# Four block pairs of the second layer by Strassen's scheme instead of three, with the sums of its first matrix formed inside the first layer's loop

## The chip, the cores and the metric

One core of one Trainium2 chip runs the whole program. Its engines are TensorE (PE in the rows, its weight loads PEld), VectorE (DVE), ScalarE (ACT), GpSimd (POOL) and SyncE (SP), which here only issues DMAs. The metric is the device time of one execution in microseconds (us), the median of the runs.

## The reference: attention in chunks, then two feed-forward layers

```python
# attention: 8 batches x 8 heads, 576 positions in chunks of 64, head_dim 64
scores = scale * np.matmul(q_c, k_c.transpose(0, 1, 2, 4, 3))
scores = scores - np.max(scores, axis=-1, keepdims=True)
attn = np.exp(scores)
attn = attn / (np.sum(attn, axis=-1, keepdims=True) + 1e-09)
out = np.matmul(attn, v_c)
x = np.ascontiguousarray(attn_out.transpose(0, 2, 1, 3)).reshape(B * S, H * D)   # 4608 tokens x 512

# first layer: rational activation, d_ff 2048
h = x @ w_in
h2 = h * h
h3 = h2 * h
P = a[0] + a[1] * h + a[2] * h2 + a[3] * h3
Q = 1.0 + np.abs(b[0]) * np.abs(h) + np.abs(b[1]) * h2
g = P / (Q + 1e-06)
return (g @ w_out).astype(np.float32)

# second layer, d_ff 2048
h = x @ w_in
r = np.maximum(h, 0.0)
g = s * (r * r) + b
return (g @ w_out).astype(np.float32)
```

## The kernel before, in words

**Tiling.** The 4608 tokens are `NB` = 9 blocks of `TB` = 512; the model width 512 is `KD` = 4 slices of 128, the width 2048 is `MF` = 16 slices of 128. Every operand of a product is held as a sum of a high and a low part (`xh`, `xl`; `gh`, `gl`; the two halves of a weight tile), so that one product of two tiles is three matmuls. The weights come from memory as 64-bit words and are put together on the chip, tile by tile: `w_stage` loads one, `w_ends` (two ACT operations, `w` and `wst`), `w_clamp` and `w_shift` (DVE), `w_top` (DVE, reads `wst` and `w`), `w_sum` (POOL), `w_hi` (ACT) and `w_lo` (DVE or POOL).

**Steps.** A step i is one slice of 128 of one block: `mm1(i)` (12 matmuls of 512 columns into one of three PSUM banks `h`), the element-wise work, and, some steps later, `mm2(i)` (12 matmuls into the accumulators `acc`). Of the first layer's element-wise work `ew_abs`, `ew_num`, `ew_ln`, `ew_exp` and `ew_hi` are on ACT, `ew_den` (two operations, `r`) and `ew_lo` (`gl`) on POOL, `ew_b` (two operations, `t`) and `ew_d` (three operations, the last writes `t` again and frees the bank `h`) on DVE. The first layer has 9 x 16 = 144 steps, the second layer has 48 such plain steps for its first three blocks. The attention of 36 tiles of 128 tokens runs ahead of the blocks that need it, between the steps.

**The other six blocks** of the second layer go in three pairs by Strassen's scheme: seven products of half-size matrices in place of eight, in each of the two multiplications. For that the 2x2 parts of the weights have to be added and subtracted first; `conv` in `finish` does it for both matrices, 8 sets of two tiles each (`kind` 0 is the first matrix, `w_in`, `kind` 1 the second), and writes the results to memory (`wq_d`), from where `wi_load` and `wo_load` fetch them. A pair has 336 matmuls in each of its two multiplications.

**What sets the order.** Each engine works its own list in order. `START` is a list written out by hand, one token an operation, up to step 33 (`BEGUN`); it holds the conversion of the 32 tiles of the first layer's weights. Then a loop in code runs steps 33 to 127, the same for each step, with one attention tile every four steps. `TURN` is again a list, up to step 165, with the conversion of the 32 tiles of the second layer. From there `finish` lets a planner with costs and due times set the order of 26 plain steps, the 16 sets of `conv` and the three pairs.

## Time and profile before

| what | value |
|---|---|
| median of 3 runs (lowest to highest) | 1665.79 us (1664.94 to 1668.18) |
| the profiled execution: its time, its span | 1667.5 us, 1665.4 us |
| granted TensorE clock over the span | 0.989 |
| busy: PE, DVE, ACT, POOL | 96%, 79%, 66%, 41% |
| the chain that ended last | PE 85%, DVE 8%, ACT 2%, issue 2%, DMA 1%, POOL 1% |
| first matmul of steps 0, 33, 48, 128, 144, 166 | 56.8, 269.2, 359.0, 830.0, 912.8, 1038.0 us |

The last row is read from the timeline of PE: the start of the first matmul on line 460 of that step. So the program has five stretches: up to 56.8 us (attention of the first tiles, no step yet), `START` up to 269, the loop up to 830, `TURN` up to 1038, and what `finish` plans. The views used are the page, busy times by stretch (a stretch's length, then for each engine the busy time and in brackets the number of instructions, then the granted clock, the DMA share and GB/s), groups of instructions by line and shape (busy time, mean ns of one, idle time of the engine before them and its releaser), and waits.

### The profile page before, as it was taken

To read this page: it belongs to the slowest core of one execution; us is meant where nothing else is said; L and a number is where in the kernel's file an instruction comes from. 1 tells how busy PE (TensorE), PEld (TensorE's weight loads), DVE (VectorE), ACT (ScalarE), POOL (GpSimd) and SP (SyncE) were. 2 spreads that over 40 slices of the span, in tenths; PEclk is the share of its full clock that TensorE was granted. 3 is DMA by queue.
4 is the path that set the end of the run, shared out by engine and by line. 5 is a ranking of instruction groups with operands and counts; after the bars stand their busy time and mean duration, and the time that the engine had idled before them with its cause. 6 is when DMAs were issued, how large, how long until landed. Compare 5 with 4: busy or idle time off the path is not lost.

```text
span 1665.4 us, 26182 instructions
## 1 busy us (share of the span) xinstructions
PE 1604.4 (96%) x9148; PEld 1313.3 (79%) x9148; DVE 1311.4 (79%) x2071; ACT 1091.3 (66%) x1824; POOL 678.1 (41%) x576
## 2 busy tenths in 40 slices
PE   4689999999999999999999999899999999999997
...
GB/s 205 160 124 115 73 55 111 34 29 64 39 57 31 60 39 33 59 31 77 33 82 112 92 127 101 276 325 246 190 252 241 194 151 276 219 222 161 286 182 67
DMA packets 339971, 217.76 MB, mean 131 GB/s; under 512 B 262528, under 2 KB 297344, under 8 KB 339840
## 3 DMA queue, kind: packets, MB, share of 16 engines
...
## 4 chain that ended last, share of the span: by engine, by line
PE 85%; DVE 8%; ACT 2%; issue 2%; DMA 1%; POOL 1%; SPq 0%; DVEq 0%; ACTq 0%; POOLq 0%
PE acc L478 27%; PE ae L1041 12%; PE h L460 9%; PE h L461 9%; PE h L462 9%; PE hA L980 8%; PE hE L980 4%; PE hc L980 2%; PE hc L1041 2%; PE pat L350 1%; PE pat L289 1%; PE pat L325 1%; DVE h L607 1%; DVE t L608 1%; DVE ah L606 1%
## 5 line engine op out<-in xcount | busy, mean ns | idle before, releaser
L460 PE MATMUL h<-xh,w 128*128 128x512 f32 x768 | 308.6, 402 | 9.3 <-DVE t L608 5.2
L462 PE MATMUL h<-xh,w 128*128 128x512 f32 x768 | 301.7, 393 | 0.0
L461 PE MATMUL h<-xl,w 128*128 128x512 f32 x768 | 301.5, 393 | 0.0
L478 PE MATMUL acc<-gh,w 128*128 128x512 f32 x1152 | 285.5, 390 | 0.6 <-ACT gh L616 0.6
L478 PEld LDWEIGHTS acc<-gh,w 128*128 128x128 f32 x1152 | 215.7, 188 | 46.0 <-ACT gh L616 1.0
L1041 PE MATMUL ae<-gs,wo 128*128 128x512 f32 x864 | 219.4, 391 | 2.3 <-DVE acc L1062 1.2
L568 POOL TENSOR_SCALAR r<-ah,ab_sb 128x512 f32<-128x512 f32 x138 | 110.1, 798 | 235.4 <-ACT ah L551 235.1
L1041 PEld LDWEIGHTS ae<-gs,wo 128*128 128x128 f32 x864 | 161.8, 188 | 38.6 <-DVE acc L1062 2.4
L571 POOL TENSOR_TENSOR r<-r,ah 128x512 f32<-128x512 f32 x140 | 182.4, 1303 | 13.8 <-ACT r L566 2.2
L460 PEld LDWEIGHTS h<-xh,w 128*128 128x128 f32 x768 | 145.7, 190 | 43.2 <-DVE t L608 8.6
L622 POOL TENSOR_TENSOR gl<-t,gh 128x512 fp32r<-128x512 f32 x129 | 167.8, 1301 | 16.2 <-ACT gh L616 14.5
L462 PEld LDWEIGHTS h<-xh,w 128*128 128x128 f32 x768 | 145.3, 189 | 31.3
L461 PEld LDWEIGHTS h<-xl,w 128*128 128x128 f32 x768 | 145.8, 190 | 29.0 <-DVE xl L366 0.5
L606 DVE SCALAR_TENSOR_TENSOR ah<-r,h 128x512 f32<-128x512 f32 x144 | 98.3, 683 | 79.3 <-ACT h L599 78.7
L478 PE MATMUL acc<-gl,w 128*128 128x512 f32 x576 | 154.2, 390 | 0.0
L980 PE MATMUL hA<-xs,wi 128*128 128x512 f32 x576 | 146.7, 390 | 0.7 <-ACT g L991 0.7
L616 ACT ACTIVATE gh<-t 128x512 fp32r<-128x512 f32 x144 | 90.8, 631 | 78.0 <-DVE t L608 71.4
L406 POOL TENSOR_TENSOR w<-w,wst 128x512 int32<-128x512 int32 x64 | 94.6, 1487 | 79.2 <-DVE w L403 48.5
L980 PEld LDWEIGHTS hA<-xs,wi 128*128 128x128 f32 x576 | 108.0, 188 | 23.7 <-ACT g L991 1.1
L478 PEld LDWEIGHTS acc<-gl,w 128*128 128x128 f32 x576 | 108.1, 188 | 22.6 <-POOL gl L622 0.3
L599 ACT ACTIVATE h<-ah,exb 128x512 f32<-128x512 f32 x144 | 99.5, 691 | 39.1 <-DVE t L590 36.6
L594 ACT ACTIVATE ah<-r,lnb 128x512 f32<-128x512 f32 x144 | 103.4, 718 | 30.3 <-POOL r L571 29.8
...
## 6 DMA issues: line engine op xcount, KB each, us to landing
wi<-wq SPq DMA_DIRECT2D x84, 512.0 KB, 4.1
wo<-wq SPq DMA_DIRECT2D x84, 512.0 KB, 4.7
...
wst<-in_moe_w_out_dram SPq DMA_DIRECT2D x30, 512.0 KB, 4.6
wst<-in_moe_w_in_dram SPq DMA_DIRECT2D x29, 512.0 KB, 5.1
...
```

Of the source, the lines that this page charges most:

```text
L460: T.matmul(h, wh, xh[:, kk], start=kk == 0, stop=False)
L461: T.matmul(h, wh, xl[:, kk], start=False, stop=False)
L462: T.matmul(h, wl, xh[:, kk], start=False, stop=kk == KD - 1)
L478: T.matmul(o, l, r, start=first and n == 0, stop=last and n == 2)
L568: eng.tensor_scalar(out=r, in0=ah, scalar1=ab_sb[:, 1:2], scalar2=ab_sb[:, 0:1], op0=ALU.mult, op1=ALU.add)
L571: eng.tensor_tensor(out=r, in0=r, in1=ah, op=ALU.mult)
L594: A.activation(tmp[i]["ah"], tmp[i]["r"], AF.Ln, scale=RS, bias=lnb)
L599: A.activation(h_t[i], tmp[i]["ah"], AF.Exp, scale=-1.0, bias=exb)
L606: V.scalar_tensor_tensor(out=t, in0=r, scalar=ONE, in1=y, op0=ALU.add, op1=ALU.mult)
L622: (eng or (G if i < N1 else V)).tensor_tensor(out=gl, in0=tmp.pop(i)["g"], in1=f(g_t[i][0]), op=ALU.subtract)
L980: T.matmul(ps[b], w[:, l, z * P:(z + 1) * P], x[:, z], start=n == 0 and p in (1, 2, 5), stop=n == 5, skip_group_check=True)
L1041: T.matmul(o, w[:, e, l, dp * P:(dp + 1) * P], gx[t, 2 * u + e, k][0][:, g], start=n == 0 and p in (1, 2, 5), stop=n == 5, skip_group_chec ...
```

## The change

- `finish` begins at step 150 and has 10 plain steps in place of 26; the second layer has 16 plain steps (block 0 alone) instead of 48, and four pairs (blocks 1 and 2 to 7 and 8) instead of three.
- The first layer's order of steps: block 0 with slices 0 to 7, block 1 with 0 to 7, block 2 with all 16, block 1 with 8 to 15, block 0 with 8 to 15, then blocks 3 to 8. Since three blocks' inputs are alive at once, that of block 0 is written to memory (`x_out`) and read back (`x_back`).
- `START` reaches to step 48; it and `TURN` are new lists, in which the parts of `att_S_out`, `att_sum`, `w_mid`, `ew_b` and `ew_d` are tokens of their own. `TURN` converts 16 weight tiles, those of `w_out`, not 32, and fetches the 16 tiles of `w_in` (`w_get`).
- The loop of steps 48 to 127 is now `LOOP`, a list of 16 steps, played five times. It holds, beside the 16 steps and four attention tiles, the conversion and the sums of two sets (four tiles) of the second layer's `w_in` (`pre_load` to `pre_put2`). There are 8 sets, so four of five passes begin two each, and the last third of a pass's second set falls into the next pass. In `LOOP` three of 16 `ew_lo` and one of four `att_norm` go to DVE (`yD`, `nD`), and three of 16 first operations of `ew_den` to ACT (`rP`).
- `conv` is left for `kind` 1 alone.

```diff
-BEGUN = 33
+BEGUN = 48
-TURN_AT, TURNED = 128, 166
+TURN_AT, TURNED, BIAS_AT = 128, 150, 21
+LOOP = (
+    "l:47 E:47 M:48 wh0:-1 ws1:-1 X:17 wk0:-1 wh1:-1 B:48 Na:47 Q:18 wp0:-1 Nb:47 wkD1:-1 Nc:47 r:48 t:48 H:47 "
...
-    for j0 in (0, NB):
-        steps += [(j0 + j, y * HF + m, m == 0, m == HF - 1) for y in range(2) for j in range(2) for m in range(HF)]
-        steps += [(j0 + j, m, m == 0, m == MF - 1) for j in range(2, NB) for m in range(MF)]
+    for j, m0, m1 in ((0, 0, HF), (1, 0, HF), (2, 0, MF), (1, HF, MF), (0, HF, MF), *((j, 0, MF) for j in range(3, NB))):
+        steps += [(j, m, m == m0, m == m1 - 1) for m in range(m0, m1)]
+    steps += [(NB, m, m == 0, m == MF - 1) for m in range(MF)]
...
-        i0, i1 = TURNED, N1 + 3 * MF
+        i0, i1 = TURNED, N1 + MF
...
-        convs = [(kind, s) for u in range(4) for kind in range(2) for s in (2 * u, 2 * u + 1)]
+        convs = [(1, s) for s in range(HF)]
...
-        PAIRS = [(3 + 2 * t, 4 + 2 * t) for t in range((NB - 3) // 2)]
+        PAIRS = [(1 + 2 * t, 2 + 2 * t) for t in range(NB // 2)]
...
+        def pre_load(s):
+            pre[s] = [big([P, TB, 2], I32, "wst", z) for z in range(2)]
+            for x, st in enumerate(pre[s]):
+                m = s + HF * x
+                SP.dma_start(
+                    out=st.rearrange("p (k f) w -> p k (f w)", k=KD),
+                    in_=w_in2[:, m * P:(m + 1) * P].bitcast(I32).rearrange("(k p) f -> p k f", p=P),
+                )
...
+        def pre_clamp(s):
+            w_clamp(None, pre[s, "w"].rearrange("p z f -> p (z f)"))
+
+        def pre_shift(s):
+            w_shift(pre[s, "w"].rearrange("p z f -> p (z f)"))
+
+        def pre_top(s, x):
+            w_top(pre[s][x], pre[s, "w"][:, x])
+
+        def pre_sum(s, x):
+            w_sum(pre[s][x], pre[s, "w"][:, x])
+
+        def pre_hi(s, x):
+            pre[s, "o", x] = big([P, 2, TB], F32R, "wp", 2 + x)
+            A.activation(pre[s, "o", x][:, 0], f(pre[s, "w"][:, x]), AF.Copy)
+
+        def pre_lo(s, x, eng):
+            o = pre[s, "o", x]
+            eng.tensor_tensor(out=o[:, 1], in0=f(pre[s, "w"][:, x]), in1=f(o[:, 0]), op=ALU.subtract)
...
+        def pre_put(s, x):
+            o = f(pre[s, "o", x])
+            SP.dma_start(out=wi_d[s + HF * x], in_=o)
+            for k, y in (((0, 0), (1, 1)), ((5, 1),))[x]:
+                SP.dma_start(out=at0(s, k), in_=o[:, :, y * 2 * P:(y + 1) * 2 * P])
+
+        def pre_mix(s, x, eng):
+            w = f(pre[s, "w"]).rearrange("p z (y c) -> p z y c", y=2)
...
+            eng.tensor_tensor(out=w[:, o[0], o[1]], in0=w[:, i[0], i[1]], in1=w[:, j[0], j[1]], op=how)
+
+        def pre_hi2(s, x):
+            pre[s, "c", x] = big([P, 2, 2, 2 * P], F32R, "wc", 3 - x)
+            A.activation(pre[s, "c", x][:, :, 0], f(pre[s, "w"][:, x]).rearrange("p (n c) -> p n c", n=2), AF.Copy)
...
+        def w_get(m):
+            hl = wp.tile([P, 2, TB], F32R, tag=f"w0_{m}", name="w0")
+            w_in[1, m] = hl[:, 0], hl[:, 1]
+            SP.dma_start(out=f(hl), in_=wi_d[m])
...
-        for i in range(BEGUN, TURN_AT):
-            mm1(i)
...
+        for z in range((TURN_AT - BEGUN) // MF):
+            rows_ = LOOP.split()
...
+            for t in rows_:
+                op, n = t.split(":")
+                tiles = op in ("X", "Q", "o", "VS", "e", "n", "nD", "A", "a", "v", "u") or op[0] in "sm"
+                n = int(n) + z * (SPB if tiles else 2 if op[0] == "w" else MF)
+                if op[0] == "w" and not 0 <= n < HF or tiles and n >= NST:
+                    continue
+                row[op](n)
```

DVE in the loop of the first layer, before (`t`, `ah`, `h` are the element-wise work of a step, `sm` belongs to an attention tile, line 606 reads `h` after ACT's exponential):

```order
L606 SCALAR_TENSOR_TENSOR ah<-r,h 128x512
L607 SCALAR_TENSOR_TENSOR h<-ah,h 128x512
L608 SCALAR_TENSOR_TENSOR t_5613<-t_5613,a_sb,h 128x512
L313 TENSOR_REDUCE sm<-e 128x8
L314 TENSOR_SCALAR sm<-sm 128x8
L315 RECIPROCAL sm<-sm 128x8
L589 TENSOR_TENSOR t_5710<-t_5710,h 128x512
L590 SCALAR_TENSOR_TENSOR t_5710<-t_5710,a_sb,h 128x512
L606 SCALAR_TENSOR_TENSOR ah<-r,h 128x512
```

The same loop on DVE now (lines 659, 679, 681, 683, 657 are the former 590, 606, 607, 608, 589; `w` is a pair of weight tiles, line 456 its clamp, 1467 one of its sums; line 697 is `ew_lo`):

```order
L659 SCALAR_TENSOR_TENSOR t_5729<-t_5729,a_sb,h 128x512
L456 TENSOR_SCALAR w<-w 128x1024
L683 SCALAR_TENSOR_TENSOR t_5620<-t_5620,a_sb,h 128x512
L697 TENSOR_TENSOR gl<-t_5600,gh 128x512
L679 SCALAR_TENSOR_TENSOR ah<-r,h 128x512
L681 SCALAR_TENSOR_TENSOR h<-ah,h 128x512
L1467 TENSOR_TENSOR w<-w 128x256
L683 SCALAR_TENSOR_TENSOR t_5729<-t_5729,a_sb,h 128x512
L349 TENSOR_REDUCE mx<-h 128x4
L349 TENSOR_REDUCE mx<-pat 128x4
L657 TENSOR_TENSOR t_5805<-t_5805,h 128x512
```

Between the operations of the steps now stand those of the weight tiles and an `ew_lo` that was POOL's.

POOL in the loop, before (`r` is `ew_den`, `gl` is `ew_lo`, `e` the attention's division):

```order
L568 TENSOR_SCALAR r<-ah,ab_sb 128x512
L571 TENSOR_TENSOR r<-r,ah 128x512
L622 TENSOR_TENSOR gl<-t_5550,gh 128x512
L568 TENSOR_SCALAR r<-ah,ab_sb 128x512
L571 TENSOR_TENSOR r<-r,ah 128x512
L622 TENSOR_TENSOR gl<-t_5613,gh 128x512
L319 TENSOR_TENSOR e<-e,sm 128x512
```

POOL in the loop now (lines 634, 637 and 697 are the former 568, 571 and 622; `wst` is the loaded word, `wp` a tile's high and low part):

```order
L634 TENSOR_SCALAR r<-ah,ab_sb 128x512
L637 TENSOR_TENSOR r<-r,ah 128x512
L466 TENSOR_TENSOR w<-w,wst 128x512 x2
L697 TENSOR_TENSOR gl<-t_5285,gh 128x512
L1450 TENSOR_TENSOR wp<-w,wp 128x512 x2
L697 TENSOR_TENSOR gl<-t_5356,gh 128x512
L634 TENSOR_SCALAR r<-ah,ab_sb 128x512
L637 TENSOR_TENSOR r<-r,ah 128x512
L1467 TENSOR_TENSOR w<-w 128x256
```

Sums and low parts of the weight tiles stand here in pairs between two steps' `r` and `gl`.

SP in the loop, before (`qk` and `vs` are the attention's inputs, `x2d` the first layer's result of a block):

```order
L232 DMA vs<-in_v_dram 64x4x64 x4
L218 DMA qk<-in_q_dram 32x8x32 x8
L218 DMA qk<-in_k_dram 32x8x32 x8
L536 DMA x2d_86<-o 128x4x64 x8
L232 DMA vs<-in_v_dram 64x4x64 x4
```

And now (line 603 is the former 536, 1419 loads a pair of weight tiles, 1457, 1459 and 1479 store its parts):

```order
L1457 DMA wi_109<-wp 128x1024
L1459 DMA wq_0_92<-wp 128x2x256
L282 DMA vs<-in_v_dram 64x4x64 x4
L603 DMA x2d_86<-o 128x4x64 x8
L1419 DMA wst<-in_moe_w_in_dram 128x4x256 x2
L1479 DMA wq_0_92<-wc 128x512 x2
L269 DMA qk<-in_q_dram 32x8x32 x8
```

The load of a pair of weight tiles stands right behind the eight stores of a block's result, whose buffers it takes over, and ahead of the next attention tile's loads.

## Rows read from the trace of the kernel before

**Rows 1.** The page, part 1: busy time, share of the span, instructions.

```profile
PE 1604.4 (96%) x9148; PEld 1313.3 (79%) x9148; DVE 1311.4 (79%) x2071; ACT 1091.3 (66%) x1824; POOL 678.1 (41%) x576
```

**Rows 2.** Busy time by stretch, two of four equal 16-step turns of the loop.

```profile
358.96:453.25 94.29, 94.29 (x657) 77.45 (x656) 75.71 (x126) 59.40 (x97) 57.28 (x52) 1.00 0.24 47
...
641.84:736.13 94.29, 94.29 (x658) 77.44 (x656) 75.69 (x126) 59.56 (x97) 57.22 (x52) 1.00 0.25 46
```

**Rows 3.** Groups by line and shape, DVE, 358.96 to 735.9 us.

```profile
L606 DVE SCALAR_TENSOR_TENSOR ah<-r,h 128x512 f32<-128x512 f32 x64 | 43.9, 685 | 47.8 <-ACT h L599 47.8
```

**Rows 4.** Busy time by stretch: plain steps in TURN, one Strassen pair.

```profile
912.76:1037.99 125.23, 125.23 (x554) 103.52 (x552) 92.19 (x120) 95.30 (x159) 75.72 (x54) 1.00 0.35 114
...
1280.00:1433.00 153.00, 152.38 (x669) 125.34 (x668) 118.96 (x178) 98.56 (x167) 0.00 (x0) 1.00 0.69 217
```

**Rows 5.** Groups by line and shape, DVE, 0 to 270 us.

```profile
L403 DVE SCALAR_TENSOR_TENSOR w<-wst,w 128x512 int32<-128x512 int32 x32 | 21.8, 722 | 0.5
...
L396 DVE TENSOR_SCALAR w<-w 128x1024 f32<-128x1024 f32 x16 | 12.7, 794 | 11.9 <-ACT w L391 11.9
L400 DVE TENSOR_SCALAR w<-w 128x1024 int32<-128x1024 int32 x16 | 12.5, 784 | 0.6
...
L417 DVE TENSOR_TENSOR w<-w,w 128x512 fp32r<-128x512 f32 x8 | 7.7, 966 | 0.0
L622 DVE TENSOR_TENSOR gl<-t,gh 128x512 fp32r<-128x512 f32 x8 | 7.5, 938 | 0.0
...
L319 DVE TENSOR_TENSOR e<-e,sm 128x512 f32<-128x512 f32 x3 | 2.9, 961 | 0.0
```

**Rows 6.** The same view, DVE, 1038 to 1150 us and 1280 to 1586 us.

```profile
L839 DVE TENSOR_TENSOR wf<-wf 128x256 f32<-128x256 f32 x52 | 19.6, 416 | 0.2
...
L1019 DVE TENSOR_TENSOR gs<-g,gs 128x512 fp32r<-128x512 f32 x112 | 72.6, 684 | 9.4 <-ACT gs L1015 9.0
```

**Rows 7.** The same view, ACT and POOL, 0 to 270 us.

```profile
L391 ACT ACTIVATE w<-wst 128x512 f32<-128x512 f32 x32 | 21.2, 664 | 11.6 <-DMA wst<-in_moe_w_in_dram 7.7 <-POOL w L417 3.0 <-DMA wst<-in_moe_w_out_dram 0.9
...
L566 ACT ACTIVATE r<-ah,ab_sb 128x512 f32<-128x512 f32 x2 | 1.6, 803 | 0.0
...
L406 POOL TENSOR_TENSOR w<-w,wst 128x512 int32<-128x512 int32 x32 | 46.4, 1464 | 37.2 <-DVE w L403 21.9 <-issue 5.4 <-ACT h L599 4.9
...
L417 POOL TENSOR_TENSOR w<-w,w 128x512 fp32r<-128x512 f32 x24 | 31.7, 1332 | 0.0
```

**Rows 8.** Busy time by stretch, three in which weights are converted beside steps.

```profile
829.96:945.49 115.53, 115.17 (x506) 94.31 (x504) 102.14 (x145) 89.31 (x148) 82.26 (x67) 1.00 0.30 97
...
120.00:260.00 140.00, 135.98 (x831) 109.76 (x829) 130.19 (x199) 101.05 (x171) 106.86 (x89) 1.00 0.29 80
80.00:140.00 60.00, 53.82 (x305) 43.04 (x306) 57.29 (x87) 45.32 (x79) 47.20 (x39) 0.93 0.37 102
```

**Rows 9.** Busy time from step 0 to 48, and PE's longest wait there.

```profile
56.83:358.96 302.13, 287.43 (x1885) 231.63 (x1886) 270.05 (x426) 210.68 (x356) 210.31 (x178) 0.98 0.34 85
...
PE h L460 <- DVE t L608: 4.8, 5, 1.3
```

**Rows 10.** PE's waits 1037.99 to 1090 us, and its timeline after the first.

```profile
PE acc L478 <- ACT o L521: 2.7, 1, 2.7
PE acc L478 <- ACT gh L616: 2.1, 1, 2.1
...
1067.71 3.29 PE L478 MATMUL acc<-w,gh 128*128 128x512 f32 x8 [2.73 <-ACT o L521]
```

**Rows 11.** DMAs by line: KB each, us to landing; SP's timeline, eight issues.

```profile
wst<-in_moe_w_in_dram SPq DMA_DIRECT2D x29, 512.0 KB, 5.1
...
x2d<-o SPq DMA_DIRECT2D x48, 128.0 KB, 2.4
raw<-x2d SPq DMA_DIRECT2D x12, 512.0 KB, 7.3
...
373.49 3.78 SPq L218 DMA_DIRECT2D qk<-in_q_dram  x8
```

More of the change, by code (lines that the diff above doesn't have):

```diff
@@ L205, in att_load_rows @@
         }
+        return att[n]
+    def att_load_rows(n, dma=SP):
+        u, s0 = rows(n, 0)
+        for x in range(2):
+            dma.dma_start(
+                out=att_new(n)["qk"][:, x].rearrange("t (h d) -> t h d", h=H),
+                in_=qkv[x][u * H:(u + 1) * H, s0:s0 + P, :].rearrange("h t d -> t h d"),
+            )
     def att_load(n):
@@ L282, in att_S @@
         qT, kT = st["qT"], st["kT"]
-        ps = st["ps"] = banks or [*map(att_banks(where), range(2))]
+        ps = st["sc"] = banks or [*map(att_banks(where), range(2))]
         for p in range(NP):
@@ L539, in store @@
                     )
[L540 removed]
+            elif jj < NB:
                 SP.dma_start(out=x2d[jj % NB][t], in_=o)
@@ L543, in store @@
                 out_store(jj, t, o)
-        halves.update(jj for jj, _, _ in sums)
         sums.clear()
@@ L785, in plain @@
             last = next((n for n in range(i - 1, i0 - 4, -1) if bank_of(n) == bank_of(i)), None)
-            xs = [f"xl{kk}" for kk in range(KD)] if jj == NB + 2 else []
-            op(f"M{i}", "T", 12 * MM, mm1_x, i, after=[f"Kr{last}", *xs])
+            op(f"M{i}", "T", 12 * MM, mm1_x, i, after=[f"Kr{last}"])
         def plain_ew(i):
@@ L1124, in m1_op @@
             if k == 1:
-                wait += [n for n in shared_c if n in plan.ops]
+                wait += [n for n in shared_c if n in plan.ops] + ["biasout" if "bias" in plan.ops else None]
+                hold["att"] = f"hs11{c}"
             n = f"P{t},{s},{k}"
@@ L1244, in finish @@
             l2(z)
-        order = plan.order({"m": 0, "s": 4, "c": 6})
+            if z == BIAS_AT:
+                op("bias", "T", 3.0, bias_mm, after=[f"c{n}cs" for n in range(nc_)] + [hold["att"]])
+                op("biasout", "V", 0.3, bias_out, after=["bias"], give=[("s", 1)])
+        order = plan.order({"m": i0 - N1, "s": 8, "c": 6})
         for n in order:
@@ new lines, in tile_chunk_attention__then__rational_ffn__then__relu2_ffn, with both, den @@
+        do["h"] = lambda n, _: w_get(n)
+        def both(n):
+            banks = [*map(att_banks("x"), range(2))]
+            att_V(n, "", banks)
+            if n + 1 < NST:
+                att_S(n + 1, "", banks)
+        def den(n, part=""):
+            for x in part or " ":
+                ew_den(n, x.strip())
+        row = {
+            "M": mm1, "B": ew_abs, "t": ew_num, "r": den, "rD": lambda n: den(n, "D"), "rP": lambda n: den(n, "ph"),
+            "l": ew_ln, "E": ew_exp, "H": ew_hi, "y": ew_lo, "yD": lambda n: ew_lo(n, V), "R": mm2,
+            "j": lambda n: evac(steps[n][0], (0, 1)), "i": lambda n: evac(steps[n][0], (2, 3)), "O": lambda n: (add(0), add(1), store()),
+            "X": att_turn, "Q": att_load, "o": att_load_v, "VS": both, "e": att_exp, "n": lambda n: att_norm(n, G),
+            "nD": lambda n: att_norm(n, V), "A": lambda n: att_A(n, "x"), "a": att_A_out, "v": att_V_hi, "u": att_V_lo,
+            "wl": pre_load, "wd": pre_clamp, "we": pre_shift,
+        }
@@ L1409, in tile_chunk_attention__then__rational_ffn__then__relu2_ffn @@
+        out_at.clear()
+        wq.extend((1, m) for m in range(MF))
         play(TURN)
```

328 lines of the change are left out of this document (165 added, 163 removed), and 132 rows, old and new, of tables (LOOP, START, TURN).

## The prediction

> **What bounds the kernel now.** I read the page first: PE is busy 96% of the span, the next engine, DVE, 79% [rows 1]. An average does not say which stretch is bound by what, so the busy times by stretch come next. A 16-step turn of the loop takes 94.29 us, each of four turns the same, and PE is busy for all of it; DVE works 75.7 us of that, ACT 59.5, POOL 57.2 [rows 2]. In the groups, DVE's idle time stands almost all in front of line 606, where it waits for ACT's exponential [rows 3]: DVE is the engine with time left and PE the one without. `TURN` and the Strassen pairs look alike: 125.23 of 125.23 us and 152.38 of 153 [rows 4]. PE loses time only before step 33 and around step 170. So a matmul removed from the full stretches is time saved, as long as the other engines still keep up; and the question is DVE in the loop.
>
> **Part 1: the matmuls removed.** Two blocks cost 2 x 16 x 24 = 768 matmuls as plain steps and 2 x 336 = 672 as a Strassen pair, so 96 matmuls of 512 columns go; the order of PE's instructions in the changed kernel confirms 6528 in place of 6624, and the attention's are the same. The price of one: 125.23 us for 23 steps' worth, 552, is 0.2269 us, and 152.38 us for the 669 recorded of a pair is 0.2278 [rows 4]. Sum: 96 x 0.227 = **21.8 us less**. The Trainium skill ("TensorE: Matmul & The Clock Gate", Back-to-back issue gap) gives an isolated gap of 512 columns by 2.4 GHz plus 2.5 ns, 0.216 us; by that the term would be an estimated 20.7 us. The rows hold weight loads too and decide.
>
> **Part 2: what the loop takes on.** Per turn of 16 steps there are now two sets, four weight tiles. On DVE, each by the duration it has in the first 270 us, where it also runs beside POOL [rows 5]: two clamps and two shifts of 1024, 2 x 0.794 + 2 x 0.784 = 3.2 us; four `w_top`, 4 x 0.722 = 2.9; one low part and one low part of the sums, 2 x 0.966 = 1.9; three `ew_lo` taken from POOL, 3 x 0.938 = 2.8; one division of the attention, 1.0; two sums of 256 columns, 2 x 0.416 = 0.8 [rows 6]. Together 12.6 us, so DVE stands at 75.7 + 12.6 = 88.3 us of 94.3, **94%**. ACT gets 16 operations of about 0.66 and three of 0.80 [rows 7], 13 us, and stands at 72.5 (77%). POOL gets four sums of 1.46, six low parts of 1.33 and six half-size sums (half of 1.33, an estimate), 17.8 us, and gives up three `gl`, three first operations of `r` and one division, about 7: 68 us (72%). No engine is over 94.3 us, so throughput alone doesn't move the turn; what can is lateness. A bank `h` is freed by the last of `ew_d`, on DVE, and three banks are all PE has, so a late DVE is PE's wait. That is just the wait that tops the list from step 0 to 48 [rows 9].
>
> How much? Three stretches of before convert weights beside steps [rows 8]: with DVE at 102.1 of 115.5 us (88%) PE lost 0.4 us of 115.5 (0.3%); at 130.2 of 140 (93%) it lost 4.0 us (2.9%); at 57.3 of 60 (95%) 6.2 us (10%), though there it also waited for the attention of the first block, and at a granted clock of 0.93. 94% lies next to the second row. But the steps there need the very weights that are converted, while the loop's conversion is needed by nobody before step 150; that speaks for the first row. I take the middle, 1.6%, 1.5 us a turn; the work is there in about 4.5 of five turns: **7 us more**, with 1 and 12 as ends (0.3% and 2.9%). A gain in the loop is excluded: PE is full there.
>
> **Part 3: START.** Up to step 48 it holds, against `START` and 15 turns of the old loop's steps, 14 more operations on DVE (five low parts, six `ew_lo`, three divisions, 0.94 to 0.97 each [rows 5]), some 13 us, and one more attention tile begun. DVE was busy 270 of 302 us there [rows 9], so 32 us were idle to take it; but PE lost 14.7 us in the same stretch, so the cover is not whole. On the other side the new order of steps needs the second half of the weights eight steps later (24, not 16), and single operations can slip between others. From -6 (the better part of the stretch's named waits gone) to +10 (most of the 13 on the path). I take **+2**. The copies of block 0's input out and back have at least eight steps, some 45 us, to hide in on the way back, at a DMA share of 0.34; four transfers of 512 KB landed in 7.3 us [rows 11].
>
> **Part 4: TURN and after.** 16 tiles are converted in 22 steps, a like density to before, at no cost: PE was full at DVE 88% [rows 8]. Eight sets of `conv` less to do by DVE and the queues. Around step 170 PE waited 2.7 us for the evacuation of a block's accumulators and 2.1 for a late `gh`, and after the first it ran slower: 8 matmuls took 3.29 us [rows 10] where 8 take 1.8, so it was at the lower of its two clock levels (1.2 against 2.4 GHz) for some 1.5 us of loss. After the change no plain block follows a plain block there, so the first wait with its slow matmuls, 4.2 us, should go; the second may stay. I take **-4** (0 to -6.5). What is late next is DVE in the first pair: eight sets and the pair's own sums, covered by 10 plain steps, in which DVE has only `ew_lo` to do. At the program's end the stores after the last matmul stay as they are.
>
> **Sum.** The profiled execution took 1667.5 us with a span of 1665.4; the median of the runs is 1665.8, 1.7 below that execution. -21.8 + 7 + 2 - 4 = -16.8, against the profiled execution 1650.7, and as a median 1665.8 - 16.8 = **1649.0 us**.
>
> **Rivals.**
> *The cover holds everywhere.* The loop stays at 94.3 us a turn: -21.8 + 1 + 0 - 4, 1641 us. For: DVE's instructions of the weights have no reader near, and the row at 88% lost next to nothing. Against: 94% is not 88%.
> *START or the pair load is late.* START at its upper end gives 1657. Or ACT stands still for the loaded words: the load waits until eight stores have been issued (eight issues took 3.8 us) and landed (2.4), and itself lands 5.1 later [rows 11], about 11 us after the evacuation, some two and a half steps; if ACT gets there 3 us early and the delay goes through to PE in four turns, 12 us: 1661. Against: ACT has over 20 us idle in a turn.
> *DVE decides the loop (the other side).* If DVE's order at 94% works like the stretch from 80 to 140 us, PE loses 10%, 9.7 us a turn, 44 us in 4.5 turns: 1665.8 - 21.8 + 44 - 4 + 2 = 1686 us. The kernel gets slower than before from 5.3 us a turn (23.8 by 4.5). Against: that stretch also waited for the attention.
> *DVE and POOL shut each other out.* Sixteen of the new DVE operations of a turn read SBUF in a way that none of the old loop's did (two inputs from SBUF, or a clamp or shift), and such an operation takes 0.94 to 0.97 us beside POOL [rows 5] and 0.684 without [rows 6]: a mean wait of 0.27 us. If each waited out a whole POOL operation of 1.33 [rows 7], 21 us, DVE would need 75.7 + 12.6 + 21 = 109 us, 15 above the turn: 67 us in 4.5 turns, 1709 us. The Trainium skill ("SBUF — State Buffer", Who interferes with whom) has the pair of ports that the two engines share as an exclusive lock for the whole instruction: by that rule such waits are to be had in any list that doesn't place the two apart. The trace agrees that there is a wait, with 0.27 us, not 1.33.
> That the change doesn't do what it says is excluded by the count of matmuls.
>
> **How the numbers follow.** Forecast (1644 to 1655): 0.45. Cover holds: 0.25. START or the loads late (up to 1661): 0.17. DVE decides the loop or the ports shut out: 0.10 and 0.03. The range takes in the cover with a START that gains 5, and the late cases, and leaves out the two last and the far tail of the first: 1636 to 1663. 0.2%, 3.3 us, is what a measurement of this kernel can tell from no change. Faster by more, under 1662.5: the first three nearly whole, 0.85; within: the upper edge of the late cases and the lower of DVE's, 0.05; slower: 0.10.
>
> **What would show it.** Right: a 16-step turn of 95 to 97 us with PE 97 to 99% and DVE about 88 us busy; PE's longest wait there on DVE's last operation of `ew_d`; step 48 at 355 to 365 us; no PE wait on an evacuation after step 150; PE's matmuls 96 fewer. Wrong: a turn of 94.3 (the cover held) or over 99; DVE's `ew_lo` and low parts over 1.2 us each (the ports); ACT waiting for the loaded words for microseconds; step 48 later than 365.

## The result, and the profile after

The kernel after takes 1646.1 us (1644.6 to 1646.9, four runs), the kernel before beside it 1666.4 (1664.9 to 1668.2): ratio 0.9877, 95% interval 0.986 to 0.9894, 20 us faster. The profiled execution took 1646.9 us, its span 1645.1 us, 20.3 less than the span of before.

The page of after, part 1, against [rows 1]:

```profile
PE 1587.8 (97%) x9052; PEld 1291.3 (78%) x9052; DVE 1338.2 (81%) x2169; ACT 1119.1 (68%) x1895; POOL 612.5 (37%) x521
```

Busy time by stretch of after: up to step 0, steps 0 to 48, the five turns of the loop, and steps 128 to 150 (length; busy us of PE, weight loads, DVE, ACT, POOL with their counts; granted clock; DMA share; GB/s):

```profile
0.00:61.09 61.09, 31.88 (x504) 25.21 (x504) 41.59 (x86) 37.69 (x73) 27.64 (x27) 0.89 0.86 215
61.09:354.44 293.35, 283.24 (x1809) 227.21 (x1809) 258.19 (x429) 217.46 (x368) 179.94 (x145) 0.98 0.37 97
354.44:452.79 98.35, 95.45 (x657) 77.07 (x656) 86.72 (x147) 66.09 (x112) 63.76 (x56) 1.00 0.39 98
452.79:548.96 96.17, 95.50 (x658) 77.06 (x656) 82.53 (x142) 68.78 (x116) 68.29 (x62) 1.00 0.48 127
548.96:644.95 95.99, 95.45 (x658) 77.05 (x657) 82.17 (x142) 68.84 (x116) 68.22 (x62) 1.00 0.48 127
644.95:740.39 95.44, 95.14 (x657) 77.13 (x656) 82.50 (x142) 68.85 (x116) 68.29 (x62) 1.00 0.49 128
740.39:835.54 95.15, 94.67 (x625) 76.74 (x624) 73.22 (x124) 61.73 (x103) 57.40 (x52) 1.00 0.27 72
835.54:958.46 122.92, 121.02 (x529) 98.64 (x528) 107.24 (x161) 100.70 (x167) 78.99 (x61) 1.00 0.49 168
```

Cut at step 48 and step 128, the 20.3 us fall into three pieces. Step 48 starts at 354.44, where before it started at 358.96: **-4.5**. The five turns take 481.1 us where four took 94.29 [rows 2] and the last 93.8, together 471.0: **+10.1**. From step 128 to the end it is 809.6 against 835.4: **-25.9**. So the loop gives back a third of what the two other pieces gain. It gives it back unevenly: 4.1 in the first turn, 1.6 a turn in the next three, 1.3 in the last.

What PE waited for in the loop of after, and below that from step 0 to 48 (us in total, times, longest):

```profile
PE h L530 <- DVE t L683: 4.1, 8, 1.8
```

```profile
PE h L530 <- DVE t L683: 6.4, 7, 3.4
PE pat L383 <- POOL e L377: 1.8, 1, 1.8
PE h L530 <- ACT xh L416: 1.1, 1, 1.1
```

One kind of wait is all that the view lists for the loop: the first matmul of a step waits for its bank, which the last part of `ew_d` (line 683, line 608 of before) of three steps earlier frees. DVE, though, is busy for only 73 to 87 us of a turn: late at single places, not full. From step 128 to the end of the plain steps PE's two longest waits are these:

```profile
PE h L530 <- DVE t L683: 0.9, 1, 0.9
PE acc L548 <- ACT o L588: 0.7, 1, 0.7
```

### The profile page after: what moved, and what is told of

It is laid out like the page before. It is cut to its first block, busy times and chain, and to the rows that moved or that the text cites. A ratio compares the mean times of both kernels' runs of the same rounds, so it can differ in the third digit from the quotient of the medians.

```text
span 1645.1 us, 26368 instructions
## 1 busy us (share of the span) xinstructions
PE 1587.8 (97%) x9052; PEld 1291.3 (78%) x9052; DVE 1338.2 (81%) x2169; ACT 1119.1 (68%) x1895; POOL 612.5 (37%) x521
## 4 chain that ended last, share of the span: by engine, by line
PE 74%; DVE 10%; ACT 5%; DMA 3%; issue 3%; POOL 2%; SPq 2%; ACTq 0%; DVEq 0%; POOLq 0%
PE acc L548 18%; PE ae L1107 16%; PE hA L1046 11%; PE h L530 6%; PE h L532 5%; PE h L531 5%; PE hE L1046 5%; PE hc L1046 3%; PE hc L1107 2%; DVE h L681 1%; DVE ah L679 1%; SPq L269 1%; DMA wst<-in_moe_w_in_dram 1%; DVE t L657 1%; DVE t L683 1%
## 5 line engine op out<-in xcount | busy, mean ns | idle before, releaser
L1107 PE MATMUL ae<-gs,wo 128*128 128x512 f32 x1152 | 293.4, 391 | 1.6 <-DVE acc L1126 0.7
L530 PE MATMUL h<-xh,w 128*128 128x512 f32 x640 | 257.4, 402 | 13.4 <-DVE t L683 11.3
L1107 PEld LDWEIGHTS ae<-gs,wo 128*128 128x128 f32 x1152 | 216.0, 188 | 49.6 <-DVE acc L1126 1.1
L531 PE MATMUL h<-xl,w 128*128 128x512 f32 x640 | 251.1, 392 | 0.3 <-DVE xl L424 0.3
L532 PE MATMUL h<-xh,w 128*128 128x512 f32 x640 | 251.1, 392 | 0.0
L1046 PE MATMUL hA<-xs,wi 128*128 128x512 f32 x768 | 195.7, 390 | 0.7 <-ACT g L1057 0.7
L530 PEld LDWEIGHTS h<-xh,w 128*128 128x128 f32 x640 | 120.9, 189 | 50.5 <-DVE t L683 19.5
L1085 DVE TENSOR_TENSOR gs<-g,gs 128x512 fp32r<-128x512 f32 x224 | 146.5, 684 | 15.0 <-ACT gs L1081 14.4
L1081 ACT ACTIVATE gs<-g 128x512 fp32r<-128x512 f32 x224 | 132.7, 624 | 28.2 <-DVE g L1077 27.9
L532 PEld LDWEIGHTS h<-xh,w 128*128 128x128 f32 x640 | 120.9, 189 | 26.0
L623 ACT ACTIVATE t<-h,a_sb 128x512 f32<-128x512 f32 x144 | 110.8, 771 | 30.5 <-PE h L532 14.5
L1128 DVE TENSOR_TENSOR acc<-ae,acc 128x512 f32<-128x512 f32 x112 | 77.0, 689 | 60.8 <-PE ae L1107 59.6
```

The lines of the kernel that those rows point to most:

```text
L530: T.matmul(h, wh, xh[:, kk], start=kk == 0, stop=False)
L531: T.matmul(h, wh, xl[:, kk], start=False, stop=False)
L532: T.matmul(h, wl, xh[:, kk], start=False, stop=kk == KD - 1)
L623: A.activation(t1, h_t[i], AF.Identity, scale=a_sb[:, 3:4], bias=a_sb[:, 2:3])
L1046: T.matmul(ps[b], w[:, l, z * P:(z + 1) * P], x[:, z], start=n == 0 and p in (1, 2, 5), stop=n == 5, skip_group_check=True)
L1081: A.activation(gx[t, s, k][0][:, 0], gt[t, s, c], AF.Copy)
```

## The experiments

All stages in one table: the start of step 48, the five turns, and from step 128 to the end, each from one profiled execution, in us; then the median of the runs and its ratio to before, with the interval. Before's median was 1667.5 to 1668.7 in these comparisons.

| kernel | step 48 | turn 1 | 2 | 3 | 4 | 5 | rest | median | ratio |
|---|---|---|---|---|---|---|---|---|---|
| before | 358.96 | 94.29 | 94.29 | 94.29 | 94.29 | 93.83 | 835.4 | 1666.4 | 1 |
| after | 354.44 | 98.35 | 96.17 | 95.99 | 95.45 | 95.15 | 809.6 | 1646.1 | 0.9877 (0.986 to 0.9894) |
| e11 after again | 351.59 | 98.41 | 96.31 | 95.84 | 95.70 | 95.12 | 809.8 | 1645.8 | 0.9871 (0.9855 to 0.9888) |
| e1 no weight work | 351.19 | 98.13 | 94.88 | 94.87 | 94.84 | 94.40 | 809.9 | 1640.2 | 0.9831 (0.9818 to 0.9844) |
| e2 less of it on DVE | 351.54 | 98.30 | 95.42 | 95.45 | 95.41 | 95.13 | 809.9 | 1643.5 | 0.985 (0.9837 to 0.9864) |
| e3 less on POOL | 350.45 | 98.70 | 95.77 | 96.05 | 95.81 | 94.82 | 810.0 | 1646.1 | 0.9865 (0.9851 to 0.9878) |
| e4 five moves undone | 350.31 | 98.70 | 96.71 | 97.60 | 96.61 | 95.59 | 809.5 | 1649.6 | 0.9883 (0.987 to 0.9897) |
| e5 no additions | 354.22 | 96.23 | 95.47 | 95.48 | 95.49 | 94.84 | 809.9 | 1642.8 | 0.9844 (0.9831 to 0.9858) |
| e6 additions on POOL | 354.73 | 96.19 | 95.88 | 96.39 | 96.39 | 94.88 | 810.0 | 1645.5 | 0.9858 (0.9844 to 0.9871) |
| e7 three places | 351.62 | 98.57 | 95.53 | 96.01 | 96.25 | 94.82 | 809.7 | 1644.4 | 0.9856 (0.9843 to 0.987) |
| e8 parts together | 373.06 | 98.33 | 96.07 | 96.17 | 95.77 | 94.92 | 808.4 | 1665.0 | 0.9981 (0.9972 to 0.999) |
| e9 other places | 351.92 | 100.15 | 95.35 | 95.37 | 95.65 | 94.73 | 809.8 | 1646.1 | 0.987 (0.9855 to 0.9884) |
| e10 all moves | 353.12 | 96.61 | 96.20 | 95.46 | 95.78 | 94.79 | 809.7 | 1643.3 | 0.9852 (0.9837 to 0.9867) |
| e12 all, two more | 352.45 | 96.20 | 95.78 | 95.79 | 95.70 | 94.21 | 809.7 | 1641.3 | 0.9841 (0.9827 to 0.9854) |

**The unchanged kernel again.** The stages can only be compared between kernels if they stay put between executions.

> The kernel after, unchanged, on the chip of the two runs beside it: its own time there, and its stages once more. In six kernels with the same first list step 48 began between 350.3 and 354.7 us. If that spread belongs to the execution and not to the kernel, it begins in that range here too, and the loop takes 481 plus or minus 0.5 us with the same turns (98.4, 96.2, 96.0, 95.5, 95.2, each within 0.5).

The turns agree within 0.3 us each and the rest within 0.3, so half a microsecond in a turn means something. Step 48 does not stay put: with the same first list up to there it starts between 350.3 and 354.7 us in ten executions (after, e1 to e7, e9, e11). A run's total carries that spread; below, the turns decide. Of before there is one trace, so its own spread up to step 48 is not known.

**What the weight work costs.** In the loop's player, rows of the list are skipped. e1 skips all of it and lets the stores write other data:

```diff
+                if op[0] == "w":
+                    if op in ("wp0", "wp1", "wP0", "wP1"):
+                        filler(n, int(op[2]), op[1] == "P")
+                    continue
                 row[op](n)
```

> Left out: all work on the first matrix of the last layer inside the loop (loads, absolute values, clamps, shifts, sums, splits); only its DMAs to memory stay, with other data, so the output is not the reference's. This prices the whole of that work. In the kernel after, the loop from step 48 to step 128 takes 481.1 us where before it took 471.0. Theory A (that work, by the instructions it puts between the older ones on DVE, ACT and POOL, costs the loop its 10 us): the turns fall to 94.2 to 94.5 us, the loop to about 471 to 473, the run to about 1637. Rival B (the rewritten order of the old instructions, the halved steps and the moved ones, costs it): the turns stay at 95 to 96, the run at about 1645. Rival C (the transfers cost it): as B, since their larger half, the stores, stays.

e2 skips on DVE `wd we wf0 wf1 wmD0 wmD3`, e3 skips on POOL `ws0 ws1 wm0 wm1 wm2 wm3`:

```diff
+                if op in ("wd", "we", "wf0", "wf1", "wmD0", "wmD3"):
+                    continue
```

> Left out: the clamp, the shift, the two word merges and two of the six sums and differences of each weight pair, that is all that the loop's weight work has on DVE, some 6.8 us a turn by its own durations; the output is not the reference's. If theory A holds by way of DVE (late results of DVE on the path of the rational function), the turns fall from 95.2 to 98.3 us to 94.5 to 95.5 and the run by 5 to 9 us, to about 1638 to 1641. If POOL's or ACT's part of that work is the cause, the run moves by less than 2 us.

> Left out: the two sums and the four mixed sums and differences of each weight pair that stand on POOL in the loop, some 9.7 us a turn of POOL; the output is not the reference's. DVE's part stays. If DVE alone is the cause, the run moves by less than 2 us (1644 to 1647). If DVE and POOL disturb each other (DVE's results come later while POOL works), or if POOL's own lateness holds the softmax and the denominators up, the run falls by 3 to 7 us, to 1639 to 1643.

Turns 2 to 4 of e1, turns 2 and 3 of e2, turns 2 and 3 of e3:

```profile
449.33:544.21 94.88, 94.75 (x658) 77.27 (x656) 74.90 (x130) 60.04 (x100) 50.53 (x46) 1.00 0.48 105
544.21:639.08 94.87, 94.74 (x658) 77.26 (x657) 74.89 (x130) 60.04 (x100) 50.58 (x46) 1.00 0.50 108
639.08:733.91 94.83, 94.69 (x657) 77.21 (x656) 74.91 (x130) 60.06 (x100) 50.56 (x46) 1.00 0.50 107
```

```profile
449.84:545.26 95.42, 95.13 (x657) 77.11 (x656) 77.07 (x132) 68.66 (x116) 67.80 (x62) 1.00 0.49 128
545.26:640.72 95.46, 95.18 (x658) 77.11 (x656) 77.12 (x132) 68.62 (x116) 67.82 (x62) 1.00 0.48 128
```

```profile
449.15:544.92 95.77, 95.50 (x657) 76.96 (x656) 83.29 (x142) 68.54 (x116) 59.44 (x52) 1.00 0.48 127
544.92:640.97 96.05, 95.67 (x657) 76.96 (x656) 83.34 (x142) 68.61 (x116) 59.44 (x52) 1.00 0.48 127
```

Theory A was half right. Of the 1.6 us that turns 2 to 4 lose (mean 95.9 against 94.29), the weight work makes 1.0 (94.9 without it); 0.6 stay. Half of these 0.6 stand at one place: PE's pause ahead of step 52, 0.30 us over the pitch, is there in every turn of after and of e1, and gone in e9 below, where an old instruction ahead of it on DVE has moved. The other half is the order's too, or that of the transfers, which e1 keeps; against the transfers speaks that e1's last turn, at 75 GB/s and not 107, loses 0.6 as well (94.40 against 93.83). DVE's ten operations a turn that e2 skips are worth 0.4 to 0.5 of the 1.0; the ten of POOL's that e3 skips are worth nothing by themselves, though POOL has 9 us less to do. The rest, 0.5, is in what e2 left: ACT's part, and two low parts on DVE (lines 1450 and 1475), which the expectation of e2 overlooked when it said "all" (it also speaks of six sums a pair, where the list has four, one of them on DVE). And the first turn does not move at all: 98.13 without any weight work. Its 4 us have another cause. Of the rivals, B holds for the first turn and, in part shown, for the third of the later ones' loss that stays; C does not explain 1.0 us a turn that go while the stores stay.

**Moving five operations back to POOL.**

```diff
+                op = {"yD": "y", "nD": "n", "rP": "r"}.get(op, op)
```

> Whole computation. The five instructions that the loop's list moved off POOL (three low parts and one division onto DVE, two denominators onto ACT and back) go back to POOL in every turn. If the change's balance was needed (POOL too full otherwise), the run is 1 to 6 us slower than the kernel after, 1647 to 1652. If DVE's load is what makes the loop late and POOL has room (72% busy), it is 1 to 3 us faster, 1643 to 1645.

```profile
449.01:545.71 96.70, 95.56 (x657) 76.97 (x656) 81.26 (x139) 66.66 (x113) 75.74 (x68) 1.00 0.48 126
545.71:643.31 97.60, 96.12 (x657) 77.15 (x656) 81.14 (x139) 66.56 (x113) 75.71 (x68) 1.00 0.47 125
```

DVE's longest wait in turns 2 to 4 of e4, then of after:

```profile
DVE ah L679 <- ACT h L668: 15.1, 22, 1.6
```

```profile
DVE ah L679 <- ACT h L668: 7.9, 16, 0.9
```

Turns of 96.6 to 97.6, 1 us longer than in after, though DVE has 1 us less to do. POOL at 75.7 of 97 us is not full either, but DVE waits twice as long for the exponential, which stands behind POOL's denominator. The moves were needed. In medians the difference (0.9883 against 0.9877) is inside the intervals; the turns show it.

**The first turn.** What stands there and in no other turn is the sum of the two halves of block 0's accumulators: four additions of 128x512 (line 597). DVE's timeline of after around PE's longest wait in the loop (start, us, line, operation, count):

```profile
376.29 0.68 DVE L679 SCALAR_TENSOR_TENSOR ah<-r,h 128x512 f32<-128x512 f32 x1
377.00 0.69 DVE L681 SCALAR_TENSOR_TENSOR h<-ah,h 128x512 f32<-128x512 f32 x1
377.73 0.75 DVE L683 SCALAR_TENSOR_TENSOR t<-t,a_sb,h 128x512 f32<-128x512 f32 x1
378.40 0.68 DVE L657 TENSOR_TENSOR t<-t,h 128x512 f32<-128x512 f32 x1
...
381.00 3.20 DVE L597 TENSOR_TENSOR o<-o 128x512 f32<-128x512 f32 x2
384.12 0.68 DVE L679 SCALAR_TENSOR_TENSOR ah<-r,h 128x512 f32<-128x512 f32 x1
384.72 0.66 DVE L371 TENSOR_SCALAR sm<-sm 128x8 f32<-128x8 f32 x1
385.41 0.20 DVE L373 RECIPROCAL sm<-sm 128x8 f32<-128x8 f32 x1
385.53 0.67 DVE L681 SCALAR_TENSOR_TENSOR h<-ah,h 128x512 f32<-128x512 f32 x1
386.24 0.75 DVE L683 SCALAR_TENSOR_TENSOR t<-t,a_sb,h 128x512 f32<-128x512 f32 x1
```

Line 683 at 386.24 is what PE's step 54 needs, and two additions of 3.20 us stand ahead of it. In before, all eight additions of that layer's two split blocks stand ahead of step 48, between 248 and 286 us; the new order of steps moved block 0's four behind it. So the first turn carries work that the first list gave up; what they cost PE in before was not measured. The additions of after in the whole program (ns, least, median, most):

```profile
L597 DVE TENSOR_TENSOR o<-o x4: 683/1094/1775, 330.6 to 382.4; 128x512 f32<-128x512 f32 x4
L597 POOL TENSOR_TENSOR o<-o x4: 1262/1518/1749, 339.0 to 385.3; 128x512 f32<-128x512 f32 x4
```

The same instruction takes 0.68 us at 330 us, when POOL has nothing of this kind, and 1.50 and 1.78 here, beside POOL's subtraction and additions, which stretch to 1.74. e5 leaves the additions out, e6 puts them on POOL one by one, where the list has weight rows that are empty in the first turn:

```diff
-            if jj in part and t // 2 == z:
+            if jj in part and jj and t // 2 == z:
```

```diff
+                for k, at in enumerate(("wm2:-1", "wm3:-1", "wH1:-1", "wK1:-1")):
+                    rows_[rows_.index(at)] = f"g:{k}"
+                rows_[rows_.index("O:47")] = "o1:47"
...
+            "g": add_one, "o1": lambda n: store(),
```

> Left out: the four additions that join the two halves of token block 0 (two on DVE, two on POOL) in the loop's first turn; the output is not the reference's. The first turn took 98.35 us in the kernel after and 98.13 us with none of the loop's weight work, the four later ones 94.4 to 96.2, so the weight work is not what makes the first one long. Theory D (the additions: DVE's two took 1.50 and 1.78 us each instead of 0.68, side by side with POOL's, and the last step of the rational function stood behind them while PE waited 2.2 us): the first turn falls by 2.0 to 2.5 us, to 95.9 to 96.4; the later turns and the rest stay. Rival E (the seam between the first list and the loop): the first turn stays over 97.5.

> Whole computation. The four additions of block 0 all go to POOL, one at a time, to four places earlier in the first turn where the list has weight work in the later turns and nothing in the first; DVE has none. Theory D: the first turn falls by 1.5 to 2.5 us to 96 to 97, the run by as much, to about 1644. If POOL's additions hold the denominators up, or if two engines on the same memory disturb each other whoever adds, the first turn stays at 98 or becomes longer.

The first turn of e5, the first turn of e6, and the additions of e6:

```profile
354.22:450.45 96.23, 95.16 (x657) 77.09 (x656) 83.56 (x145) 66.30 (x112) 60.50 (x54) 1.00 0.40 100
```

```profile
354.73:450.92 96.19, 95.12 (x658) 77.12 (x656) 83.16 (x145) 66.25 (x112) 65.42 (x58) 1.00 0.40 100
```

```profile
L595 POOL TENSOR_TENSOR o<-o x4: 1282/1297/1299, 372.6 to 379.8; 128x512 f32<-128x512 f32 x4
```

Theory D holds: 2.1 and 2.2 us of the first turn are the additions, and it is enough to take them off DVE; kept apart from DVE's they take 1.28 to 1.30 us each, not up to 1.75. But e6 kept 1.4 of the 2.2: its turns 3 and 4 are 0.4 and 0.9 us longer than after's, while in e5 the later turns, in which nothing was left out, became shorter, 95.5. How late the engines enter a turn seems to carry over into the next; that was not taken further.

**Place or load.** Four kernels move instructions in the list; e7 and e9 leave the load as it is, e10 and e12 also have the additions on POOL. e7:

```diff
-    "... sa:17 l:50 bb:50 M:51 sc:17 y:49 ..."
+    "... sa:17 l:50 M:51 sc:17 bb:50 y:49 ..."
-    "E:51 Na:51 wP1:-1 mb:17 wKD0:-1 ... wP0:-1 mc:17 Nb:51 ... Nc:51 r:53 ba:53"
+    "E:51 Na:51 wP1:-1 mb:17 ... mc:17 Nb:51 ... Nc:51 r:53 wKD0:-1 wP0:-1 ba:53"
-    "... ba:56 wa0:1 M:57 mb:18 l:55 E:55 r:56"
+    "... ba:56 M:57 mb:18 l:55 E:55 wa0:1 r:56"
```

> Whole computation. Three instructions of the loop's list change place: the low part of a mixed weight on DVE goes behind the last step of the rational function of step 51 (with the store that follows it), the absolute value of the next weights on ACT behind the exponential of step 55, and the second product of step 50 on DVE behind the subtraction that frees the bank of step 52. Theory A in its narrow form (the weight work costs the loop by single instructions that stand ahead of the one PE waits for, not by the engines' load): the waits of PE ahead of steps 52, 54 and 58 (0.30, 0.33 and 0.53 us over the pitch of 0.227) go, the turns fall by 0.4 to 0.9 us each, the run by 2 to 4 us. If the load as such is the cause, the waits come back elsewhere and the turns stay within 0.2 us.

The wait ahead of step 54 went in turns 2 to 5, the one ahead of 52 grew (0.30 to 0.43 us over the pitch), the one ahead of 58 stayed, and the loop took 481.2 us, no less than before the moves. e9 follows those two waits to what really stands behind them:

```diff
-    "sa:17 l:50 bb:50 M:51 sc:17 y:49 wm3:-1 sb:17 u:16"
+    "sa:17 l:50 M:51 sc:17 u:16 bb:50 y:49 wm3:-1 sb:17"
-    "R:52 wk0:0 y:53 wp0:0 wp1:0 t:55 Na:54 r:55 X:19"
+    "R:52 y:53 wp1:0 t:55 Na:54 r:55 wk0:0 wp0:0 X:19"
-    "wm0:0 B:56 ... M:57 mb:18 l:55 E:55 r:56 ... wm1:0 Na:55 l:56"
+    "wm0:0 l:55 B:56 ... M:57 mb:18 E:55 wa0:1 Na:55 r:56 ... wm1:0 l:56"
```

> Whole computation. The run before this one moved three instructions and gained nothing in the loop: the wait ahead of step 54 went, but the one ahead of step 52 grew from 0.30 to 0.43 us over the pitch, since the last reader of its bank is the low part of the attention's output on DVE, and the one ahead of step 58 stayed at 0.46, since POOL's two weight low parts (2.55 us) stand ahead of the denominator of step 55. Here, besides the first two moves that stay (the mixed weight's low part behind step 51, the absolute value behind the exponential of step 55): that low part of the attention's output comes ahead of the product of step 50, the second weight low part on POOL behind the denominator of step 55, and step 55's logarithm, exponential and first last-step earlier. If the loop's loss is single instructions in the wrong place, turns 2 to 5 fall to 94.9 to 95.3 us, the run by 3 to 4 us. If it is the load in that stretch (DVE and POOL busy without a pause for some 10 us), the waits move on to the steps behind and the turns stay over 95.5.

Turns 2 and 3 fell to 95.4, 0.6 to 0.8 less, turn 4 did not (95.65), with the waits ahead of 52 and 58 gone and the one ahead of 54 grown to 0.6. But in the first turn DVE came 0.7 us later still to the bank of step 54, and that cost more than 0.7. Busy time and PE's timeline of e9 there:

```profile
381.90:384.90 3.00, 0.41 (x3) 0.01 (x1) 2.87 (x6) 0.75 (x2) 3.00 (x3) 0.94 0.23 87
384.90:387.70 2.80, 2.80 (x7) 2.22 (x8) 2.18 (x4) 2.80 (x6) 2.57 (x3) 0.50 0.86 293
387.70:390.00 2.30, 2.30 (x13) 1.95 (x12) 1.62 (x3) 2.27 (x4) 1.31 (x1) 0.95 0.45 70
```

```profile
384.89 0.80 PE L530 MATMUL h<-xh,w 128*128 128x512 f32 x1 [2.59 <-DVE t L683]
385.49 0.63 PE L531 MATMUL h<-xl,w 128*128 128x512 f32 x1
385.91 0.63 PE L532 MATMUL h<-xh,w 128*128 128x512 f32 x1
```

After a pause of 2.6 us the granted clock is 0.50 for the next 2.8 us: matmuls start 0.43 us apart instead of 0.23. In after the same wait, 1.8 us, has no slow matmuls behind it. So the first turn is 1.8 us longer, and e9 as a whole gains nothing. e10 adds e6's additions and, at the end of the first list, step 47's products ahead of a softmax sum:

```diff
-    "... s16c e16 m16a r47 m16b m16c b47a b47b n16D y46D "
+    "... s16c e16 r47 b47a b47b m16a m16b m16c n16D y46D "
```

> Whole computation. The moves of the run beside it, the additions of block 0 on POOL at four earlier places, and at the end of the first list the products of step 47 on DVE ahead of the three steps of a softmax sum (PE waited 1.1 us over the pitch ahead of step 50 there). Expected from the parts: the first turn 98.4 down to 95.0 to 96.0, the later ones 94.9 to 95.3, the loop 475 to 477 instead of 481, the run about 1640, faster than the kernel after by 4 to 6 us. If load and not place decides, about 1643 to 1645.

The loop takes 478.8 us, 2.3 less (of which 1.7 in the first turn), and the kernel 1643.3; the wait ahead of step 50 falls from 1.1 us to 0.5. That misses what place was to give, 475 to 477 and 1640, and lies where load was to leave the run, at 1643 to 1645. e12 takes up the wait ahead of step 54:

```diff
-    "ba:52 B:52 bb:51 R:48 e:17 r:51 wK1:-1 r:52 l:51 H:50"
+    "ba:52 bb:51 R:48 e:17 r:51 wK1:-1 l:51 B:52 r:52 H:50"
-    "E:51 Na:51 wP1:-1 mb:17 ... mc:17 Nb:51"
+    "E:51 mb:17 mc:17 Na:51 wP1:-1 ... Nb:51"
```

> Whole computation: the kernel of the run before with all moves, and two more for the wait ahead of step 54, which stayed (0.85 us from end to end of the pitch, in each turn). There ACT stood 1.75 us at the absolute value of step 52, whose tile DVE frees late, with the logarithm of step 51 behind it, and DVE's third last-step of step 51 stood behind two small softmax steps, one of which took 0.58 us beside POOL. Now step 51's logarithm comes ahead of that absolute value, and the two small steps ahead of step 51's first last-step. If place decides, the wait ahead of step 54 goes in every turn (0.6 us each), turns 2 to 5 fall to 94.9 to 95.2, the loop from 478.8 to 475 to 476.5, the run to about 1640. If it comes back at another step, the loop stays over 478.

```profile
352.45:448.65 96.20, 95.26 (x658) 77.04 (x657) 83.75 (x144) 65.91 (x112) 65.43 (x58) 1.00 0.40 100
448.65:544.43 95.78, 95.19 (x658) 77.18 (x657) 83.01 (x142) 68.45 (x116) 68.73 (x62) 1.00 0.48 127
544.43:640.21 95.78, 95.44 (x657) 77.29 (x656) 82.77 (x142) 68.59 (x116) 68.68 (x62) 1.00 0.48 127
640.21:735.91 95.70, 95.43 (x657) 77.28 (x656) 82.96 (x142) 68.57 (x116) 69.18 (x62) 1.00 0.48 127
735.91:830.12 94.21, 94.21 (x626) 76.79 (x624) 73.88 (x124) 61.46 (x103) 57.90 (x52) 1.00 0.27 72
```

The wait ahead of step 54 is gone in turns 2 to 5, and the loop takes 477.7 us, between the two expectations: part came back ahead of steps 55, 58 and 63. The last turn, where there is less weight work, runs at 94.2 with PE busy all of it. e12 is the fastest kernel here that does the whole computation, 1641.3 us (1639.7 to 1641.6) against 1645.8 for after; the intervals of the two ratios, 0.9827 to 0.9854 and 0.9855 to 0.9888, just don't meet. With nearly the same load, the moves were worth some 3.5 of the 10 us: 2.2 in the first turn, whose additions went from DVE to POOL, and 0.9 in the last. Turns 2 to 4 kept theirs (95.8 against 95.9; 95.5 in e9). Place moves single waits by 0.3 to 0.8 us, but none of the four kernels won back the 1.0 us that the weight work costs these turns (e9 0.4). Whether load makes it or the right places were not found stays open.

**The first list.** Why is step 48 early, with more operations on DVE than before? e8 puts the parts of `ew_d`, of the products and of the softmax steps together again, at the place of the last part of each:

```diff
-    "... N10a H9 G19 r11 ... N10b n10 N10c ..."
+    "... H9 G19 r11 ... n10 N10 ..."
```

> Whole computation. In the list up to step 48 the parts of the rational function's last steps (three), of its products (two) and of the softmax's steps (four and three), which the change can place one by one, stand together again at the place of the last part; everything else as in the kernel after. Theory F (the first list became 4.5 us shorter to step 48 because its finer steps let DVE serve PE in time): step 48 starts 4 to 10 us later (at 356 to 364) and PE's waits on DVE's last step grow by as much. Rival G (it became shorter because DVE and POOL have 12 and 30 us less to do in it): step 48 moves by less than 2 us.

Steps 0 to 48 of e8, then of e11; and PE's waits there in e8 (its line numbers are 11 lower):

```profile
60.89:373.06 312.17, 289.27 (x1809) 229.25 (x1809) 269.89 (x430) 217.20 (x368) 181.90 (x145) 0.97 0.34 91
```

```profile
61.21:351.59 290.38, 280.87 (x1809) 226.26 (x1809) 258.07 (x429) 217.16 (x368) 180.34 (x145) 0.99 0.37 97
```

```profile
PE h L519 <- DVE t L672: 14.1, 13, 4.3
PE h L519 <- DVE e L345: 4.0, 1, 4.0
```

Theory F holds in its direction, and by more than expected; rival G alone is out, since e8 too has less to do on DVE and POOL. Step 48 comes 18.6 us later than in after, 21.5 later than in e11, and the whole change shrinks to 0.9981. Of PE's 18.8 us more from step 0 to 48, 12.8 are pauses (its wait on DVE's last step grew from 6.4 to 14.1 us) and 6.0 are longer busy time, at a granted clock of 0.97 and not 0.98.

The rows tell part of why. The same instructions (430 and 429) keep DVE busy 269.9 us when they stand together and 258.1 when they are spread. Of these 11.8 us, 5.4 are longer single instructions (their durations add up to 288.1 and 282.7 us); the other 6.3 are overlap that is lost. In the timeline of after above, line 681 starts 0.71 us after line 679, whose result it needs, and 683 starts 0.73 after 681; line 657, which needs neither, starts 0.67 after 683, before 683's 0.75 us are over. Over the three middle turns the medians are: an instruction that reads what the one just ahead of it on DVE wrote starts 0.035 us after that one's end, one that does not starts 0.083 before it, 0.12 us between the two. In three turns of before the two products and the three parts of `ew_d` stood back to back in all 144 cases; in three turns of after in 75. From step 0 to 48, 174 instructions of e8 start 0.02 to 0.06 us after the end of the one ahead, as dependent ones do, against 78 of e11: 96 times 0.12 is about 11 us of DVE's time. That the place of the last part, too, makes e8 slow is likely and was not tried apart, so the 18.6 us are no price of the finer steps alone.

## Why the prediction was right or wrong

**Part 1 and part 4: right, as a sum.** From step 128 on 25.9 us went; 21.8 was forecast for the matmuls and 4 for the waits. PE's count fell by 96 as said. The wait for a block's evacuation of 2.7 us with the slow matmuls behind it [rows 10] is gone; the 0.7 us that is left of such a wait falls ahead of step 150, and no wait from step 128 on is over 0.9. PE's rows from step 128 to the end, before and after, split the sum:

```profile
829.96:1665.38 835.42, 818.92 (x3589) 672.69 (x3587) 627.21 (x950) 549.40 (x918) 152.19 (x113) 1.00 0.60 190
835.54:1645.11 809.57, 796.46 (x3493) 653.88 (x3491) 631.33 (x963) 529.71 (x893) 78.99 (x61) 1.00 0.67 209
```

PE's busy time fell by 22.5 us with 96 matmuls, its idle time from 16.5 to 13.1.

**Part 2: the right size for the wrong reason, and one place missed.** The sum put DVE at 88.3 of 94.3 us; it was 82.4. The operations were counted rightly, and by their own durations there they take 11.5 us a turn, near the 12.6. The step that failed is adding durations to busy time: durations of neighbours overlap, and the change's list also pulled the old, dependent neighbours apart (e1, without the weight work and with four more operations on DVE than before, is busy 74.9 us a turn, before 75.7), so busy time rose by 6.7 us over [rows 2]. At that share, 86%, the row at 88% in [rows 8] would have given 0.3%. Turns 2 to 4 lost 1.7%, so DVE's share did not tell the loss. 1.0 of the 1.6 us is the weight work, by place or by load; the other 0.6, at least half of it the order of the old instructions, the forecast priced at nothing. The first turn, 4.1 us, was not in the sum at all. It holds work that no other turn holds, the additions (2.2) and the seam to the first list (a wait of 1.1, 0.6 of it removable), and the prediction multiplied one turn by 4.5. Term: 7 forecast, 10.1 measured, inside its ends.

**Part 3: wrong in sign.** +2 was taken, -4.5 measured in the profiled execution, -4.2 to -8.6 over the ten. The step that failed is "14 more operations, some 13 us": the count was nearly right (502 instructions on DVE up to step 48 became 515; two of block 0's additions, which left for the first turn, were not counted), but their durations add up to only 5.1 us more (324.5 and 329.6), and DVE's busy time there fell from 307.1 to 299.8 us, by the same overlap as in part 2, which no row of before had been read for. The sentence that "single operations can slip between others" named the mechanism and gave it no price; e8 prices it, together with the places of the parts, at some 19 us.

**The errors cancelled.** 3 too little for the loop, 6.5 too much for the first list: 1649.0 against 1646.1. That the total came so near is in part luck; parts 1 and 4 are not.

**The rivals.** The cover did not hold (turns of 95.2 to 98.4). DVE did not decide the loop as at 95%. The loaded words were not late: ACT stood idle ahead of their operations for 1.3 us in the whole loop, 0.8 at most. The ports: the collision is real, but hits few instructions. The additions stretched from 0.68 to 1.78 us, and in the three middle turns a word merge (line 463) took 0.68 us in the median and 1.13 at most. The Trainium skill ("SBUF — State Buffer", Who interferes with whom) says that a VectorE instruction with two SBUF inputs contends with a GpSimd instruction that reads SBUF, and calls the port pair that they share an exclusive lock. The added 0.8 to 1.1 us are less than one of POOL's instructions (1.28), which agrees with a wait for the rest of one. Most pairs do not meet in this list: `ew_lo` on DVE, feared at over 1.2, took 0.69, but the one low part on line 1450 took 1.10 in each of the three turns.

**What would show it.** Turns of 95 to 97 came in four of five, PE's only wait on the last part of `ew_d` as said; DVE at 88 was wrong; step 48 was at 350 to 355, just ahead of the range given.
